# A linear-attention kernel with a gated output: a new order table, engine choices and PSUM banks for the same operations

## The chip, the cores and the metric

The kernel runs on one core of one Trainium2 chip. The metric is the device time of one execution in microseconds (us), lower is better. A core has five engines that each work through a queue of their own in order: TensorE (PE in the profile, with its weight loads as PEld), VectorE (DVE), ScalarE (ACT), GpSimd (POOL) and SyncE (SP), the last used here for issuing transfers. They meet only through semaphores. An instruction whose semaphore is not yet there holds up everything behind it in its queue.

## The reference

Eight batches of attention with a feature map, then a gated linear layer:

```
proj = x @ w_phi;  proj -= max|proj|;  phi(x) = [exp(proj), exp(-proj)]     # for q and k, 64 -> 128 features
kv  = phi(k)^T v;   z = sum phi(k)                                          # per batch and head
x   = phi(q) kv / (phi(q) z + 1e-6)                                         # (8, 576, 512)
gate = sigmoid(causal convolution of x, 5 taps);  out = ((x @ w_val) * gate) @ w_out
```

There are 8 batches, 8 heads, 576 rows, head width 64. Inputs and output are float32, the kernel computes in bfloat16 with float32 accumulation.

## The kernel before, in words

The kernel keeps everything of a batch on the chip. The rows of a batch are cut into 18 chunks of 128, and these into five units (four of 4 chunks, one of 2). A Python function `build` lists the work of all batches as tasks (1064 of them): each has a kind, a batch, the engine or engines that can do it, and the group of PSUM banks that it opens or uses. `build` itself fixes no order. Three tables do that:

- `ORDER` is the list of task numbers in the order in which they are written out. Each engine's queue is that list, cut down to the engine's own tasks.
- `FLEX` gives the engine (A, D or P for ACT, DVE, POOL) of each task that more than one engine can do, in order of task number.
- `BANKS` gives the PSUM banks, of 8, of each group. A group of two banks is read as one two-row block.

`WARM` adds idle matmuls (a 128x512 product of ones that nobody reads, L481) ahead of the places of `ORDER` that it names ("place:bank:count"), and before the change there are also 14 `warm` tasks of two such matmuls each. The durations in `build` (0.44, 2.22 and so on) are a planner's; nothing reads them when the kernel is built.

The stages of one batch, with the lines of the profile:

| stage | TensorE | who takes it on |
|---|---|---|
| k | `kp`: projection of kT (L555) | DVE maximum MK (L562), ACT two exps per unit into KTIL (L572), then `ek`: ACT exp of the maxima (L581) |
| v, kv | `st`: 36 matmuls per call, four calls (L598) | before it `vs`: v times EK into VT (L588, L589; 4 per batch, POOL or DVE); after it `kv`: copy of the sums (L606 DVE, L610 ACT) |
| q | `qm`: projection of qT (L555), `mqt`: transpose (L631), `qp`: projection again, minus the maximum (L642, L649) | DVE maximum MQP (L562), `mqr` (L634), ACT two exps per unit into QTIL or QTT (L657, L660) |
| x | `num`: five per batch (L670, L677), `xtp`: transposes (L699, L703) | DVE `nrm` (L688, L691), `xtc` copy into XT (L711, L716), POOL `halo` (L720) |
| gate, val | `gate` (L732, L739), `val` (L751) | ACT `tanh` (L743), DVE `gv` (L757), POOL `gvc` (L763) |
| out | `out` (L775) | `oev`: ACT (L612) or DVE (L608), store issued on SP (L797 and following) |

TensorE works with four shapes of its array here: 128x128 (`num`, `out`, transposes, idle matmuls), 64x128 (`kp`, `qm`, `qp`, `st`, `val`), 128x64 (first part of `gate`, the small fifth `num` and third `xtp`) and 64x64 (second part of `gate`).

Batches overlap: while batch b is in its gate and out stages, b+1 is in its x stage and b+2 in its k and q stages. The opening is different. k and q of batch 0 come as float32 in pieces through SP, and TensorE transposes them (`tp32`, L514). k and q of batch 1 are two transfers that POOL's queue issues (L528), q first, then k, then `w_val` (L445), then q of batch 2; they land in the tile QTIL as bfloat16, and TensorE transposes them too (`tp16`, L533). From batch 2 on the transposes are transfers (L543). In POOL's queue before the change stand, behind these loads: `c_eb` (L442), the first two `vs` of batch 0 with the load of k of batch 2 between them, the gate's weights `c_gt` (L472 to L477), the other two `vs` of batch 0, then batch 1.

In TensorE's queue before the change the transposes of k of batch 1 stand behind all five `qm` of batch 0, behind three of its `qp` and four `qm` of batch 1.

Of the kernel before, what the change touches and what calls it, by code (L numbers as in the profile page):

```python
# [25 lines left out]
PEB = 1  # L26
XB = (6, 7)
NO = 6
NW = 14
NJ = 2 * NC  # L30
XH = R // 2
HALO = 16
XW = HALO + XH
WARM = (
    "8:7:5 21:7:1 214:5:1 "
)
STD = 1.18
E1 = D + 1
QW = 2 * NR

ORDER = (
    "15 16 18 17 20 19 22 21 24 35 23 37 26 25 36 39 57 27 38 59 41 32 34 170 40 43 61 60 33 172 55 42 73 74 64 47 171 174 58 "
    "193 311 49 63 44 0 28 76 62 56 50 29 48 65 93 75 45 94 67 53 91 66 54 30 46 92 51 68 97 173 31 89 98 77 188 90 184 52 "
    "185 95 194 96 69 186 189 72 79 5 187 99 228 2 71 100 229 104 313 190 105 70 226 80 9 106 227 101 78 1 103 234 191 110 "
    "175 235 192 10 111 230 178 102 182 179 183 107 112 231 180 108 195 312 11 181 232 109 84 233 81 197 203 82 206 196 6 85 "
    "113 83 314 204 198 8 7 114 199 12 201 319 236 237 205 86 200 320 115 238 202 207 87 210 4 88 116 239 208 315 14 240 118 "
    "117 316 209 211 119 122 212 128 317 241 129 215 242 123 217 124 318 214 125 120 130 213 176 131 243 321 216 329 121 13 "
    "332 3 322 126 331 177 127 132 218 324 330 354 433 434 219 323 355 247 221 248 435 139 220 352 140 353 250 141 436 252 "
    "358 359 149 222 251 249 325 437 150 133 327 356 134 357 244 438 135 246 360 361 223 326 245 333 224 439 136 225 328 137 "
    "265 335 362 266 142 138 363 334 337 143 145 144 338 336 151 339 367 152 440 369 146 253 340 370 254 441 368 267 268 255 "  # L50
    "341 259 442 372 269 256 261 343 260 364 371 443 262 147 366 444 342 148 450 365 446 447 263 452 154 449 445 451 166 155 "
    "257 264 562 448 563 258 458 565 167 344 459 453 347 485 564 345 461 273 346 274 486 454 460 348 455 270 275 477 478 162 "
    "456 271 566 481 457 158 482 163 479 272 480 376 159 349 377 160 483 284 484 378 156 462 350 161 464 285 373 465 351 157 "
    "276 374 567 463 277 487 286 466 488 568 375 467 279 278 492 569 287 379 493 280 153 380 288 281 468 570 494 282 289 164 "
    "573 283 571 577 575 391 472 578 295 576 299 392 165 296 574 393 572 579 290 469 685 686 394 300 606 470 580 607 395 381 "
    "688 471 495 687 382 385 473 496 307 386 497 608 308 581 383 583 609 387 303 584 388 489 304 384 689 291 491 582 389 490 "
    "292 498 604 390 499 474 605 475 500 585 476 610 588 405 611 399 406 690 400 586 410 407 401 691 396 587 411 501 397 612 "
    "503 414 692 613 398 502 589 402 415 591 614 403 693 408 590 404 615 293 592 616 409 593 297 510 618 595 301 506 511 168 "
    "412 617 507 294 696 413 622 298 699 729 812 813 516 730 302 624 425 416 169 594 517 504 623 814 426 421 698 505 518 619 "
    "422 519 815 508 621 697 599 512 429 620 513 727 816 430 509 628 596 629 520 431 728 731 600 630 597 694 625 732 598 735 "  # L60
    "432 627 514 736 417 626 515 712 733 418 695 715 601 734 714 700 602 702 713 521 603 524 703 522 817 527 523 701 525 528 "
    "530 526 818 529 531 704 532 737 705 708 819 537 711 738 707 539 538 820 709 535 706 305 540 633 710 427 536 739 423 716 "
    "533 634 309 740 722 306 631 534 741 748 428 632 856 750 745 424 935 857 541 643 746 635 936 310 644 639 723 747 636 542 "
    "937 640 749 751 645 637 646 753 938 558 543 638 647 752 823 559 717 854 862 641 826 863 939 546 855 825 724 718 642 547 "
    "860 725 861 554 726 824 742 555 858 744 719 859 827 720 743 828 940 651 721 648 941 652 649 662 653 650 754 829 419 663 "
    "654 548 755 830 831 556 655 832 756 942 420 656 766 549 864 833 767 760 757 557 550 834 865 943 835 761 821 768 837 660 "
    "544 769 560 551 758 770 661 838 869 759 657 870 836 822 664 944 871 866 665 658 868 762 666 763 659 867 872 545 667 979 "
    "873 839 980 764 561 677 842 945 765 874 673 678 840 981 674 780 982 843 675 771 841 850 781 679 772 985 782 774 986 552 "
    "676 773 977 775 978 950 680 776 777 844 953 954 553 778 955 785 779 952 669 786 668 951 783 845 670 956 671 789 784 957 "
    "875 672 790 849 983 877 846 984 946 847 876 787 848 949 878 788 851 880 947 962 791 879 852 965 804 853 948 963 958 987 "  # L70
    "805 883 959 964 796 988 966 884 881 960 972 893 882 887 797 894 889 961 885 888 992 973 989 994 886 890 798 895 800 896 "
    "991 891 799 808 801 993 897 968 892 974 967 990 1001 975 1002 998 976 681 1003 809 999 969 682 810 995 1000 970 907 996 "
    "971 904 908 997 905 792 811 909 1004 906 1006 1005 793 1012 1007 1010 1016 1013 1008 916 1011 898 1009 1017 1014 901 917 "
    "1018 899 902 1019 910 1015 903 794 900 1020 806 914 683 911 795 912 802 807 1024 913 684 1021 915 803 1025 1027 1026 "
    "1030 1028 1031 1022 1029 923 1032 1037 924 1023 925 1033 1039 926 1034 1035 1040 1038 927 919 928 1036 931 929 920 1041 "
    "1054 932 918 921 930 1046 933 1055 922 1058 1056 1047 934 1042 1048 1059 1062 1057 1060 1050 1043 1049 1051 1044 1063 "
    "1052 1061 1045 1053 "
)
FLEX = (
    "ADAADAAAAAPPAPPDAAAADDAADAPPDPPDDAAADPPDPPDDADAPPAPPDAAAAAPPAPPDAADDPPAPPAAADADPPDPPDDADAPDDPPADDDDA"  # L80
)
BANKS = (
    "460006544445500124166757234523230145452301456767723672301674501445674652345230145234501276045505450101236723016701016767"
    "674230145670101011236736601674501014523236503323016723674501454567232370123456723450124567741230123236745236732374567452"
    "323450123452367010016767230167676452322367450167016767453636623674567452301452301454500101010101232320101732014501676767"
    "010122154523230145674545676767454450145674545450012303223672301010145236636423236745456701010145014524523670167452323457"
    "201230145450123457466234567014567230123674545701672301672345230177674501234545016744555"
)


# [66 lines left out]
def build(plan, em=None):  # L157

    def fn(name, *a):
        if em is None:  # L160
            return None
        f = getattr(em, name)
        return lambda t: f(t, *a)

    A = plan.add
# [5 lines left out]

    ceb = A("lv", 0, 0, "POOL", 2.6, fn("c_eb"), rank=-800)
    hold = None

    for i in range(NW):
        A("warm", 0, i, "PE", 0.44, fn("warm2"), [], plan.group("warm", 1), 0)

    for b in range(B):

# [122 lines left out]
        for c in range(5):  # L302
# [5 lines left out]
            if c in (1, 3, 4):  # L308
                i = c // 2
# [43 lines left out]
class Emit:  # L353
# [125 lines left out]

    def warm(self, bank):  # L480
        self.nc.tensor.matmul(self.PS[:, bank, :], self.ONES[:, 0:P], self.ONES[:, :], start=True, stop=True)  # L481

    def warm2(self, t):
        for _ in range(2):
            self.warm(t.grp.banks[0])

    def hold(self, t, u):
        self.nc.gpsimd.tensor_copy(self.HOLD[:, :], self.XN32["k"][:, u * 9 * D:u * 9 * D + 1])
# [317 lines left out]
@with_exitstack  # L806
def kernel(
    ctx: ExitStack,
    tc: tile.TileContext,
    q: bass.AP,  # L810
    k: bass.AP,
    v: bass.AP,
    w_phi: bass.AP,
    moe_w_val: bass.AP,
    moe_conv_w: bass.AP,
    moe_w_out: bass.AP,
    out: bass.AP,
):
    nc = tc.nc
    with tc.manual_schedule(engines=None):  # L820
        em = Emit(nc, tc, ctx, q, k, v, w_phi, moe_w_val, moe_conv_w, moe_w_out, out)
        plan = build(Plan(), em)
        warm = {}
        for x in WARM.split():
            i, bank, n = x.split(":")
            warm[int(i)] = (int(bank), int(n))
        for i, t in enumerate(plan.follow()):
            for _ in range(warm[i][1] if i in warm else 0):
                em.warm(warm[i][0])
            if t.fn is not None:  # L830
                t.fn(t)
# [30 lines left out]
```

## Time and profile before

| | |
|---|---|
| time, three runs | 229.36, 230.55 (median), 231.44 us |
| the profiled execution: its span, first to last instruction | 233.1 us |
| its own time | the page gives no other than the span |
| instructions | 9168 |
| busy: PE, DVE, ACT, POOL | 211.9 (91%), 176.4 (76%), 181.7 (78%), 103.0 us (44%) |
| mean granted TensorE clock | 0.990 |
| transfers | 39.87 MB, mean 171 GB/s |

Busy time is the union of an engine's instructions. For TensorE it counts the time from a matmul's start to its modelled end, and these overlap, so a busy TensorE need not be one at its peak; the time from one task's start to the next one's start says more. In timelines a row merges neighbours of one kind: start in us from the span's start, us taken, engine, line, operation, output<-inputs, how many, and in brackets the idle time just before with what ended it.

### The profile page before, as it was taken

The numbers are of one execution on the slowest core, as the hardware profiler recorded it, in microseconds if no ns is written. First come the engines' busy times: TensorE is split into PE (matmuls) and PEld (weight loads), VectorE is DVE, ScalarE is ACT, GpSimd is POOL, SyncE is SP. The second block draws the span as 40 slices with busy tenths as digits, with TensorE's granted clock in tenths as the row PEclk, the third lists the DMA queues.
The fourth block names the chain that finished last, engine by engine and source line by source line (L and its number), as shares of the span: only waits on it lengthen the run. The fifth ranks groups of instructions, "written<-read, shape, count | busy, mean of one in ns | idle before, by whom it ended". The sixth has DMA issues, their size and how long they took to land.

```text
span 233.1 us, 9168 instructions
## 1 busy us (share of the span) xinstructions
PE 211.9 (91%) x4027; PEld 145.5 (62%) x4027; DVE 176.4 (76%) x264; ACT 181.7 (78%) x267; POOL 103.0 (44%) x158
## 2 busy tenths in 40 slices
PE   7888997699998999999998599999999999999990
PEld 3566555567676576666766367676665867676640
DVE  2569776998789877998899549796888899583361
ACT  2878999799899987998898479978998999913320
POOL 2715992694059329800495006940009739100020
PEclk9999999999999999999999979999999999999999
DMA  6999935999699779968999981969984106156156
GB/s 199 338 257 272 208 55 160 209 181 174 116 207 242 127 160 178 302 114 114 229 167 296 167 232 30 148 126 229 263 277 143 52 3 139 37 83 204 45 177 184
DMA packets 49426, 39.87 MB, mean 171 GB/s; under 512 B 33706, under 2 KB 38826, under 8 KB 49322
## 3 DMA queue, kind: packets, MB, share of 16 engines
q1 hardware_dynamic: 43136, 29.63, 52.4%
q0 software_dynamic: 5760, 9.31, 23.8%
q8 instruction: 31, 0.51, 0.8%
q10 hardware_dynamic: 490, 0.35, 0.5%
q14 instruction: 9, 0.07, 0.1%
HBM read 30.49 MB, written 9.44 MB: 171 GB/s over the span
## 4 chain that ended last, share of the span: by engine, by line
PE 59%; DVE 16%; DMA 6%; POOL 5%; issue 5%; ACT 4%; ACTq 1%; SPq 1%; DVEq 0%
PE PS L751 12%; PE PS L775 10%; PE PS L732 7%; PE PS L555 7%; PE PS L598 6%; DVE MK L562 4%; DMA kT<-KQN 4%; DVE XN L691 4%; PE PS L670 3%; DVE MQP L562 3%; PE PS L739 3%; POOL VT L588 3%; PE PS L642 3%; DMA KTIL<-in_k_dram 2%; DVE GV L757 2%
## 5 line engine op out<-in xcount | busy, mean ns | idle before, releaser
L588 POOL TENSOR_TENSOR VT<-VN,EK 128x1152 bf16<-128x1152 f32 x31 | 65.9, 2125 | 66.5 <-ACT EK L581 55.5
L572 ACT ACTIVATE KTIL<-PS 128x1024 bf16<-128x1024 f32 (+1 forms) x80 | 72.4, 946 | 6.5 <-PE PS L555 4.3
L657 ACT ACTIVATE QTIL<-PS 128x1024 bf16<-128x1024 f32 x64 | 62.5, 1035 | 3.7 <-PE PS L649 3.3
L562 DVE TENSOR_REDUCE MQP<-PS 128x8 f32<-128x1024 f32 (+1 forms) x40 | 44.2, 1113 | 6.6 <-PE PS L555 5.5
L562 DVE TENSOR_REDUCE MK<-PS 128x8 f32<-128x1024 f32 (+1 forms) x40 | 43.9, 1111 | 4.4 <-PE PS L555 4.0
L751 PE MATMUL PS<-XT,WV 64*128 64x288 bf16 x512 | 35.5, 283 | 0.4 <-DVE XN L691 0.2
L757 DVE SCALAR_TENSOR_TENSOR GV<-TH,PS 128x576 bf16<-128x576 bf16 x32 | 23.7, 752 | 15.4 <-PE PS L751 10.5
L743 ACT ACTIVATE TH<-PS 128x576 bf16<-128x576 f32 x32 | 20.2, 654 | 16.6 <-PE PS L739 16.4
L775 PE MATMUL PS<-WOUT,GV 128*128 128x512 bf16 x128 | 31.7, 380 | 0.0
L751 PEld LDWEIGHTS <-WV 64*128 64x128 bf16 x512 | 24.8, 94 | 8.0 <-issue 2.4
L598 PE MATMUL PS<-VT,KTIL 64*128 64x65 bf16 x1152 | 24.5, 191 | 5.1 <-issue 3.5
L598 PEld LDWEIGHTS <-KTIL 64*128 64x128 bf16 x1152 | 21.4, 95 | 8.0 <-issue 5.2
L691 DVE TENSOR_TENSOR XN<-PS,RCP 128x512 bf16<-128x512 f32 x32 | 22.1, 692 | 1.1
L732 PE MATMUL PS<-XT,GF 128*64 128x288 bf16 x256 | 21.5, 301 | 0.3 <-DVE MQP L562 0.2
L670 PE MATMUL PS<-KV,QTIL 128*128 128x65 bf16 x512 | 20.1, 193 | 1.5 <-DVE GV L757 0.5
L670 PEld LDWEIGHTS <-QTIL 128*128 128x128 bf16 x512 | 18.2, 97 | 5.0 <-issue 2.7
L612 ACT ACTIVATE OUTS<-PS 128x512 f32<-128x512 f32 x22 | 13.3, 605 | 9.6 <-PE PS L775 9.1
L775 PEld LDWEIGHTS <-GV 128*128 128x128 bf16 x128 | 11.0, 97 | 11.6 <-issue 1.1
L720 POOL COPY XT<-XT 128x224 bf16<-128x224 bf16 x8 | 3.0, 375 | 34.2 <-DVE XT L716 22.3
L555 PE MATMUL PS<-W,kT 64*128 64x128 bf16 x288 | 15.4, 225 | 2.8 <-ACT kT L522 1.0
L732 PEld LDWEIGHTS <-GF 128*64 128x64 bf16 x256 | 13.2, 112 | 4.5 <-issue 2.0
L555 PE MATMUL PS<-W,qT 64*128 64x128 bf16 x288 | 15.1, 222 | 0.8 <-ACT TH L743 0.6
(76 smaller groups left out, 265.6 us busy)
## 6 DMA issues: line engine op xcount, KB each, us to landing
VN<-in_v_dram SPq DMA_DIRECT2D x8, 1152.0 KB, 6.9
out_dram<-OUTS SPq DMA_DIRECT2D x31, 256.0 KB, 3.2
KQN<-in_q_dram POOLq DMA_DIRECT2D x6, 576.0 KB, 6.8
KQN<-in_k_dram POOLq DMA_DIRECT2D x6, 576.0 KB, 8.0
KTIL<-in_k_dram SPq DMA_DIRECT2D x4, 288.0 KB, 4.1
KTIL<-in_q_dram SPq DMA_DIRECT2D x4, 256.0 KB, 4.2
out_dram<-OUTS SPq DMA_DIRECT2D x14, 64.0 KB, 2.8
QTIL<-in_q_dram POOLq DMA_DIRECT2D x1, 576.0 KB, 9.4
```

Source lines behind the costliest of these rows:

```text
L555: nc.tensor.matmul(self.PS[:, t.grp.banks[par], i * P:(i + 1) * P], X[rows, (c0 + i) * P:(c0 + i + 1) * P], self.W2[rows, :], start=True, ...
L562: self.nc.vector.tensor_reduce(o, self.two(t.grp, n * P).rearrange("p a (c f) -> p a c f", f=F), AX.X, ALU.max, apply_absolute_value=True)
L572: self.nc.scalar.activation(self.KTIL[b % 2][:, s, c0:c0 + n, :, :].rearrange("p c a f -> p a c f"), self.two(t.grp, n * P).rearrange("p a ...
L588: eng.tensor_tensor(self.VT[g][:, s, :, 0:D], self.VN[b % 2][:, NC * g:NC * g + NC, :], e.to_broadcast([P, NC, D]), ALU.mult)
L598: nc.tensor.matmul(self.PS[:, t.grp.banks[ab], (s * 2 + x) * E1:(s * 2 + x + 1) * E1], self.KTIL[b % 2][rows, s, J // 2, J % 2, :], self.V ...
L657: self.nc.scalar.activation(o, i, AF.Exp, scale=1.0 - 2.0 * s)
L670: nc.tensor.matmul(self.PS[:, t.grp.banks[h // 4], (h % 4) * E1:(h % 4 + 1) * E1], Q[:, s, c % 2, h, (c // 2) * P:(c // 2 + 1) * P], self. ...
L691: nc.vector.tensor_tensor(o.rearrange("p (g h) d -> p g h d", g=ng), n[:, :, :, 0:D], rc.unsqueeze(3).to_broadcast([P, ng, 4, D]), ALU.mult)
L732: self.nc.tensor.matmul(self.PS[h2 * D:(h2 + 1) * D, t.grp.banks[par], 0:R], self.GF[:, h, i, :], X[:, h, :, HALO - 8 * s:HALO - 8 * s + X ...
L751: nc.tensor.matmul(self.PS[:, t.grp.banks[par], 0:R], self.WV2[rows, h, j * P:(j + 1) * P], X[rows, h, :, HALO:XW], start=(h == 0), stop=( ...
L757: nc.vector.scalar_tensor_tensor(out=self.GV[b % 3][:, j, :, :], in0=self.TH[j][:, :, :], scalar=1.0, in1=self.two(t.grp, R), op0=ALU.add, ...
L775: nc.tensor.matmul(self.PS[:, t.grp.banks[0], :], lhsT, self.WOUT[:, j, :], start=(j == 0), stop=(j == 3))
```

## The change

The operations stay the same, and so do the functions that write them out. New are:

- `ORDER`, for the same tasks without the 14 `warm` tasks (1050 tasks; their numbers shift by 14).
- `FLEX`: the copies of transposed k and q of batch 0 and 1 go 10 to DVE and 6 to ACT (before 5 and 11), all 32 `vs` to POOL (before 31, one to DVE), `kv` 9 to DVE and 7 to ACT (before 10 and 6), `oev` 13 to DVE and 23 to ACT (before 14 and 22; one of DVE's is shared between both).
- `BANKS`: a group of two is now any two banks (0 and 5, 1 and 6), before always neighbours (0 and 1, 2 and 3).
- `WARM`: 14 idle matmuls at five places, where there were 35 (7 in `WARM`, 28 in `warm` tasks).

In TensorE's queue the last transposes of k of batch 1 (units 16 to 18 and 8 to 16 of its chunks) now stand behind the `kp` and one `qm` of batch 0 and all its transposes but one, ahead of the other four `qm` of batch 0, of their transpose and of all `qp`. In POOL's queue the load of k of batch 2 moves ahead of `c_eb`, and the four `vs` of batch 0 stand together, ahead of `c_gt`. In SP's queue the two transposing transfers of batch 2 move ahead of the load of v of batch 2. At the end, the eviction of the last `out` goes to ACT, behind the other last evictions and the two stores that ACT issues.

```diff
-NW = 14
...
 WARM = (
-    "8:7:5 21:7:1 214:5:1 "
+    "3:0:6 107:5:3 125:0:2 136:6:2 159:5:1 "
 )
 ORDER = (
-    "15 16 18 17 20 19 22 21 24 35 23 37 26 25 36 39 57 27 38 59 41 32 34 170 40 43 61 60 33 172 55 42 73 74 64 47 171 174 58 "
...
+    "1 2 3 10 4 5 12 6 7 8 9 20 21 23 24 156 158 160 11 43 45 46 25 26 14 22 13 15 18 19 44 27 47 49 297 51 54 16 17 35 299 "
+    "52 59 60 50 48 36 29 30 41 31 28 39 32 179 61 33 34 53 55 58 40 57 79 80 159 168 169 0 166 167 62 37 38 56 64 83 84 197 "
...
 FLEX = (
-    "ADAADAAAAAPPAPPDAAAADDAADAPPDPPDDAAADPPDPPDDADAPPAPPDAAAAAPPAPPDAADDPPAPPAAADADPPDPPDDADAPDDPPADDDDA"
+    "ADDDDADAADPPDPPDADAADADDADPPDPPADADADPPAPPADAAAPPDPPAAADAAPPAPPDADADPPAPPDDADDDPPAPPDAAAAPPDPPDAADAA"
 )
 BANKS = (
-    "460006544445500124166757234523230145452301456767723672301674501445674652345230145234501276045505450101236723016701016767"
...
+    "014454450523670167232405350301141432534160513351722405662041627162704045740307540470671316275604352624253401035360517273"
...
-    for i in range(NW):
-        A("warm", 0, i, "PE", 0.44, fn("warm2"), [], plan.group("warm", 1), 0)
...
-    def warm2(self, t):
-        for _ in range(2):
-            self.warm(t.grp.banks[0])
```

## The prediction

> **What bounds the kernel now.** I read first the page's busy slices (each digit is the busy tenths of 5.8 us), then the shares of the chain that ended last.
>
> ```profile
> PE   7888997699998999999998599999999999999990
> ...
> DVE  2569776998789877998899549796888899583361
> ACT  2878999799899987998898479978998999913320
> ...
> PEclk9999999999999999999999979999999999999999
> ...
> PE 59%; DVE 16%; DMA 6%; POOL 5%; issue 5%; ACT 4%; ACTq 1%; SPq 1%; DVEq 0%
> ```
>
> TensorE is full from about 75 us on, DVE and ACT are nearly full up to slice 35, and the chain runs mostly over TensorE. Next, the timeline of TensorE, for what a task really takes from its start to the next one's start:
>
> ```profile
> 196.14 0.75 PE L598 MATMUL PS<-VT,KTIL 64*128 64x65 bf16 x36
> 196.73 0.27 PE L642 MATMUL PS<-qT,W 64*128 64x256 bf16 x2
> ...
> 200.33 0.75 PE L598 MATMUL PS<-VT,KTIL 64*128 64x65 bf16 x36
> 201.02 1.17 PE L732 MATMUL PS<-XT,GF 128*64 128x288 bf16 x16
> ```
>
> The same 36 matmuls take 0.59 us ahead of a task of the same array shape and 0.69 ahead of another shape. All kinds show this step: `out` 0.86 and 0.96, `kp` 0.22 and 0.33, `val` 0.98 and 1.09. So a change of shape costs 0.10 us. Counted in the order of the built program, TensorE changes shape 204 times before and 167 times after.
>
> With such start-to-start times, where nothing waits, I add up each queue: full `kp` and `qm` 0.22, `qp` 0.44, `st` 0.58, `num` 0.49, `val` 0.98, `out` 0.86, `gate` 0.51+0.15, big transposes 0.44, an idle matmul 0.215, each shape change 0.10; ACT's exps 0.90 (short ones about 0.5), DVE's maxima 1.13 and 0.60, `nrm` 0.84, `gv` 0.66. TensorE has 196.7 us of work before and 188.5 after, ACT 170.8 and 170.2, DVE 168.3 and 165.6. TensorE is the bound, with some 10% of room on ACT and DVE.
>
> I cut the run at the end of `num` of batch 1 (L670, 67.5 us). From there TensorE has 147.3 us of work and is done at 227.6: 160.1 us, 12.8 of them lost. The largest loss is one hole:
>
> ```profile
> 128.38 0.67 PE L598 MATMUL PS<-VT,KTIL 64*128 64x65 bf16 x31
> 131.92 0.25 PE L598 MATMUL PS<-VT,KTIL 64*128 64x65 bf16 x5 [2.87 <-issue]
> ```
>
> TensorE stops inside a task for 2.9 us with nothing to wait for that the profile shows, and then runs at half clock for 3.4 us (the 7 in PEclk): about 4.7 us. The rest, 8.1, is small waits. That hole may be this execution's own. Its span alone, 233.1 us, is above the runs' median of 230.55, and above the slowest run. I work out a difference against 233.1, take the hole as equal on both sides, and apply the difference to the median.
>
> **Part 1: the opening, +8.0 us.** The new order puts the transposes of k of batch 1 ahead of four `qm` and every `qp` of batch 0. When does that k land? From the page's issues and the timeline:
>
> ```profile
> QTIL<-in_q_dram POOLq DMA_DIRECT2D x1, 576.0 KB, 9.4
> QTIL<-in_k_dram POOLq DMA_DIRECT2D x1, 576.0 KB, 17.5
> WV<-in_moe_w_val_dram POOLq DMA_DIRECT2D x1, 512.0 KB, 18.7
> ...
> 8.41 0.75 POOL L528 DMA_DIRECT2D QTIL<-in_k_dram  x1
> ...
> 26.73 0.56 PEld L533 LDWEIGHTS <-QTIL 128*128 128x128 bf16 x10
> ```
>
> Issued at 8.41 it lands at 25.9; before, the transposes stood far enough back to run at 26.7 and did not wait. The change leaves every transfer ahead of it as it was (pieces of k and q, two loads of v, q), so I keep 25.9. In the new queue TensorE reaches these transposes at about 14 us: its work up to there is 8.0 us, plus the waits of the old opening. ACT and DVE have copies of those transposes early in their queues and block as well, by about 16 us. By 25.9 the old order has done all maxima of batch 0 and three of the exps of its q; the new one has one of the maxima of q and no exp of it.
>
> From 25.9 on, the new queues in order. ACT resumes at 27.1 with the copy. From it to the last exp of q of batch 0 stand 15.5 us (8.3 of them q exps of batch 0, 4.6 k exps of batch 1 that now stand ahead of them); about 1.2 us more go to waiting for the maximum of q, as DVE does its part only now. So these exps end at 43.8, before at 37.2. The `kp` that needs their banks stands in front of two `st`, so these end near 45.2, their copy on DVE at 46.5, and `num` of batch 0 begins near 47 (before 39.1). ACT's next 20.6 us, to the copy of batch 1's sums, end at 64.4; DVE then has 10.6 us up to the last `nrm` of batch 1. So `num` of batch 1 ends near 75.5 (67.5 before): +8.0. POOL doesn't decide: four `vs` from 29.1 at 2.2 us each, with 0.7 of waiting, end at 39.0.
>
> Bounds: k lands between its neighbours in POOL's queue, q at 17.1 and `w_val` at 27.8. That makes part 1 -0.8 to +9.9. I keep 25.9, its own row.
>
> **Part 2: TensorE's work behind that point, -5.1 us.** 147.3 becomes 142.2. Shape changes left fall from 139 to 112, 2.7 us. The other 2.4 us is work that the new order has done by then: a `val`, a `qp`, two and a half `kp`, a transpose.
>
> **Part 3: losses behind that point, +1.0 us.** Between the ends of `num` of batches 1 and 5 TensorE's queue held 91.4 us against ACT's 79.2 before; after it is 82.9 against 79.2. The cover for ACT's delays shrinks from 12.2 to 3.7. Bounds from the old run: 2.7 us lost in 140 to 220 us and 4.9 in 60 to 120 give 4.8 and 11.6 us over 142, against the 8.1 without the hole: -3.3 to +3.5. I take +1.0, as the margin is more like the second stage's.
>
> **Part 4: the end, +1.3 us.** Before, the last two evictions are on DVE and ACT with the stores spread:
>
> ```profile
> 226.59 1.49 ACTq L803 DMA_DIRECT2D out_dram<-OUTS  x2
> 228.18 0.38 ACT L782 ACTIVATE OUTS<-PS 128x256 f32<-128x256 f32 x1 [1.62 <-DVE OUTS L781]
> 228.59 0.57 ACTq L795 DMA_DIRECT2D out_dram<-OUTS  x1
> ```
>
> The last store is issued 3.2 us after the matmuls of the third last `out` end (225.9). After the change a whole eviction (0.60) and its store on SP (0.56) stand behind these three, all in one row: 0.6+1.5+0.4+0.6+0.6+0.6 and gaps make 4.5 us. Bounds 0 to +1.6.
>
> **Costed at nothing.** The 21 idle matmuls taken out (4.5 us of TensorE): nearly all stand in 1 to 47 us, where the next task waits for ACT, DVE or a transfer. All `vs` on POOL: batch 7's four take 8.8+0.3 us after `ek` where the old split took 8.6, and TensorE has 13 us of queued work over that stretch. Earlier transposing transfers of batch 2: they wait for k at 33.4 and end near 42, ahead of the delayed rest; without the delay they would gain up to 4 us. Copies moved between ACT and DVE: under 2 us on each, inside the delay.
>
> **Sum.** 8.0 - 5.1 + 1.0 + 1.3 = +5.2 us: a span of 238.3 instead of 233.1, a time of 235.8 instead of 230.55.
>
> **Rivals.** *The new order runs dense* (not slower). The place is ACT's and DVE's queues from 26 us on. My +8.0 holds some 4 us of waits that I put together by hand. DVE's queue alone, from 26.2 without a wait, reaches the last `nrm` of batch 1 after 45.1 us, at 71.3: +3.8. With losses behind at the best old rate (-3.3) the sum is 3.8-5.1-3.3+1.3 = -3.3: 227.3. It breaks even when these waits and losses together come out 5.2 us below mine. For it: the order is drawn from measured durations, and ACT's queue is short enough. Against it: the thin margin of part 3.
>
> *k comes earlier.* Below a landing at 20.7 us the wait no longer costs more than the rest gains; at q's 17.1 the sum is -3.6: 227.0. Nothing that shares the transfers moves, so this is unlikely.
>
> *Half clock stays.* The rows show TensorE slow at first whatever PEclk says: 8 matmuls of L555 took 0.61 us at 13.0 and 0.40 at 18.8. After the 10 us hole it starts slow again. If it stays so up to the first `num`, its 14.3 us of queued work there take 28.6, 7 more than the time there is: 242.8. For it: the idle matmuls that filled this stretch are mostly gone. Against it: in the row above 3.4 us at half clock was all that a hole cost. The Trainium skill (TensorE: Matmul & The Clock Gate, What's actually happening) says that an idle window of about 3.4 us halves the clock and that only a sustained busy one restores it. The hole above, 2.9 us and then half clock, agrees with the first half of it. By that rule the slow stretch could last as long as TensorE keeps waiting; one run of matmuls, as before, would end it.
>
> **How the numbers follow.** The sum above 0.57 (own range 232 to 241), dense order 0.25, earlier k 0.06, half clock 0.12. A measurement of this kernel tells about 1% (2.3 us) from no change. Dense order and earlier k give most of faster (0.21), their upper ends and the lower end of the sum give same (0.15), the rest is slower (0.64). The range reaches from the dense case to the half clock: 227 to 243.
>
> **What would show it.** Right: TensorE, ACT and DVE all idle from about 16 to 26 us and released by the transfer of k; q exps of batch 0 ending near 44; `num` of batch 1 ending near 75; TensorE needing 150 us from there. Wrong: no hole at 16 to 26, or `num` of batch 1 ending before 71, or fewer than 145 us behind it.

## The result, and the profile after

| | before | after |
|---|---|---|
| time, median of 4 runs each | 229.96 us (229.26 to 231.44) | 531.03 us (528.05 to 532.2) |
| profiled execution: span | 233.1 us | 530.4 us |
| busy PE, DVE, ACT | 211.9, 176.4, 181.7 us | 313.6, 180.6, 189.7 us |
| mean granted TensorE clock | 0.990 | 0.627 |

After against before is a ratio of 2.307 (95% interval 2.295 to 2.319). The forecast was 235.8 us, range 227 to 243. Direction right, size not at all. The ratios of experiments 1, 5 and 6 leave out executions more than 1.5% above the fastest of their kernel, so they can differ from the ratio of the medians. In the changed kernel's profile a line number is that of before less 9 (less 5 up to L476).

From the page of the changed kernel, the busy slices that answer to those shown of before (one digit is now 13.3 us):

```profile
PE   7136455544477666555575566765555656557784
...
DVE  5252232423334442332343323333333332223430
ACT  6142543432235432423244434143331341342223
...
PEclk9555555555557676556568655685576665557898
```

No engine is full anywhere, and that from the first slices to the last. DVE and ACT do the same work in about the same time (4 and 8 us more) and wait for the rest. TensorE is busy 102 us longer: its mean granted clock is 0.627, so each matmul takes longer (L742 `val` 381 ns on average, 283 before). It still stands idle for 217 of 530 us. The chain of waits is of no use here: it breaks off after 2% of the span.

The exps of k, from the page of before and then from that of the changed kernel, show the same busy time and the same mean, and the idle time ahead of them grown from 6.5 to 101.6 us:

```profile
L572 ACT ACTIVATE KTIL<-PS 128x1024 bf16<-128x1024 f32 (+1 forms) x80 | 72.4, 946 | 6.5 <-PE PS L555 4.3
L563 ACT ACTIVATE KTIL<-PS 128x1024 bf16<-128x1024 f32 (+1 forms) x80 | 72.4, 938 | 101.6 <-PE PS L546 33.0
```

The wait that the prediction was about is there, and it is small. The timeline just behind it shows what is not in the prediction:

```profile
25.08 1.25 PE L524 MATMUL PS<-ident,QTIL 128*128 128x128 bf16 x10 [10.65 <-DMA QTIL<-in_k_dram]
...
27.91 0.69 DVE L553 TENSOR_REDUCE MQP<-PS 128x4 f32<-128x512 f32 x1 [0.97 <-ACT KTIL L563]
...
28.65 0.61 PE L546 MATMUL PS<-W,kT 64*128 64x128 bf16 x8 [0.83 <-DVE MQP L553]
...
29.03 0.31 PE L546 MATMUL PS<-W,qT 64*128 64x128 bf16 x1
29.36 2.00 ACT L563 ACTIVATE KTIL<-PS 128x1024 bf16<-128x1024 f32 x3 [0.78 <-PE PS L546]
30.43 0.58 PE L546 MATMUL PS<-W,qT 64*128 64x128 bf16 x7 [1.09 <-ACT KTIL L563]
...
31.12 1.23 DVE L553 TENSOR_REDUCE MQP<-PS 128x8 f32<-128x1024 f32 x1 [1.92 <-PE PS L546]
...
32.39 0.61 PE L546 MATMUL PS<-W,qT 64*128 64x128 bf16 x8 [1.38 <-DVE MQP L553]
```

Read the three engines in turn. The `kp` of unit 3 of batch 1 (28.65) starts when DVE ends a maximum of q of batch 0 (27.91 + 0.69 = 28.60). The next `qm` does one matmul at 29.03 and its other seven at 30.43, behind an exp of k on ACT. The `qm` after it (32.39) starts when DVE ends the maximum before (31.12 + 1.23 = 32.35). None of these tasks needs the other's data, and none shares a bank with it: `kp` writes banks 2 and 7, the maximum read 1 and 4; the first `qm` writes 0 and 3, the exp read 2 and 7; the second `qm` writes 1 and 4, the maximum read 0 and 3. Each pair of banks lies across the other. The split `qm` shows the edge: its first matmul goes to bank 0, outside of 2 to 7, and runs; its second goes to bank 3, inside, and waits. The engines work one after another, in steps of about a microsecond, and the busy slices stay low to the end of the run.

Over the whole run the waits of TensorE add up from many short ones (us in total, times, longest):

```profile
PE PS L546 <- ACT KTIL L563: 11.7, 10, 2.0
PE PS L524 <- DMA QTIL<-in_k_dram: 10.7, 1, 10.7
PE PS L742 <- DVE MK L553: 10.6, 5, 3.9
```

`val` (L742) reads XT and WV and needs no maximum of k, yet waits 10.6 us for one. In one of the five cases (1.4 us) the maximum had read the very banks that `val` then writes. In the other four (9.3 us) they share no bank. The longest:

```profile
401.18 0.36 PE L742 MATMUL PS<-XT,WV 64*128 64x288 bf16 x1
...
404.19 1.23 DVE L553 TENSOR_REDUCE MK<-PS 128x8 f32<-128x1024 f32 x1 [2.00 <-ACT QTIL L648]
405.46 0.90 PE L742 MATMUL PS<-XT,WV 64*128 64x288 bf16 x6 [3.93 <-DVE MK L553]
```

This `val` writes banks 0 and 4, the maximum reads 2 and 5. Its first matmul goes to bank 0 and runs; its second goes to bank 4, between 2 and 5, and waits.

The semaphore waits in the built programs say the same. Before, of 849 waits of tasks with PSUM banks, 7 are for a task that neither gives them data nor shares a bank (false waits, from here on). After it is 379 of 813.

**Theory 1.** A group of two is read as one strided access, `PS[:, a:b+1:b-a]`. The software that places the semaphores takes it as an access to all banks from a to b. With neighbours that is exact. With banks 2 and 7 it is six banks, and a task waits for every user of 3 to 6 as well. **Theory 2:** the new order of the tasks starves the engines. **Theory 3:** with too few idle matmuls TensorE falls to half clock and stays there. **Theory 4:** banks far apart are slow for the chip itself.

### The profile page after: what moved, and what is told of

Read it like the earlier page. It is cut to its first block, busy times and chain, and to the rows that moved or that the text cites. A ratio compares the mean times of both kernels' runs of the same rounds, so it can differ in the third digit from the quotient of the medians.

```text
span 530.4 us, 9138 instructions
## 1 busy us (share of the span) xinstructions
PE 313.6 (59%) x4006; PEld 204.0 (38%) x4006; DVE 180.6 (34%) x265; ACT 189.7 (36%) x264; POOL 104.6 (20%) x160
## 5 line engine op out<-in xcount | busy, mean ns | idle before, releaser
L563 ACT ACTIVATE KTIL<-PS 128x1024 bf16<-128x1024 f32 (+1 forms) x80 | 72.4, 938 | 101.6 <-PE PS L546 33.0
L553 DVE TENSOR_REDUCE MQP<-PS 128x8 f32<-128x1024 f32 (+1 forms) x40 | 44.2, 1116 | 75.0 <-PE PS L546 37.3
L742 PE MATMUL PS<-XT,WV 64*128 64x288 bf16 x512 | 56.9, 381 | 21.3 <-DVE MK L553 10.6
L742 PEld LDWEIGHTS <-WV 64*128 64x128 bf16 x512 | 35.8, 123 | 36.5 <-issue 25.1
L766 PE MATMUL PS<-WOUT,GV 128*128 128x512 bf16 x128 | 45.8, 511 | 5.1 <-ACT KTIL L563 1.3
L589 PE MATMUL PS<-VT,KTIL 64*128 64x65 bf16 x1152 | 34.1, 230 | 24.5 <-ACT QTIL L648 7.2
L589 PEld LDWEIGHTS <-KTIL 64*128 64x128 bf16 x1152 | 31.5, 121 | 27.5 <-issue 14.6
L723 PE MATMUL PS<-XT,GF 128*64 128x288 bf16 x256 | 31.5, 390 | 16.9 <-DVE MQP L553 5.7
L661 PE MATMUL PS<-KV,QTIL 128*128 128x65 bf16 x512 | 28.9, 223 | 16.8 <-ACT QTIL L648 7.6
L633 PE MATMUL PS<-qT,W 64*128 64x512 bf16 (+1 forms) x80 | 24.0, 526 | 22.9 <-ACT QTIL L648 10.6
L546 PEld LDWEIGHTS <-qT 64*128 64x128 bf16 x288 | 14.4, 119 | 37.0 <-issue 36.7
L723 PEld LDWEIGHTS <-GF 128*64 128x64 bf16 x256 | 18.7, 141 | 24.5 <-issue 20.6
L679 DVE RECIPROCAL RCP<-PS 128x8 f32<-128x8 f32 (+1 forms) x40 | 8.0, 201 | 57.2 <-PE PS L661 30.8
```

Source lines behind the costliest of these rows:

```text
L546: nc.tensor.matmul(self.PS[:, t.grp.banks[par], i * P:(i + 1) * P], X[rows, (c0 + i) * P:(c0 + i + 1) * P], self.W2[rows, :], start=True, ...
L553: self.nc.vector.tensor_reduce(o, self.two(t.grp, n * P).rearrange("p a (c f) -> p a c f", f=F), AX.X, ALU.max, apply_absolute_value=True)
L563: self.nc.scalar.activation(self.KTIL[b % 2][:, s, c0:c0 + n, :, :].rearrange("p c a f -> p a c f"), self.two(t.grp, n * P).rearrange("p a ...
L589: nc.tensor.matmul(self.PS[:, t.grp.banks[ab], (s * 2 + x) * E1:(s * 2 + x + 1) * E1], self.KTIL[b % 2][rows, s, J // 2, J % 2, :], self.V ...
L633: nc.tensor.matmul(self.PS[:, t.grp.banks[par], 0:n * P], self.W2[rows, :], X[rows, c0 * P:(c0 + n) * P].rearrange("p (y h x) -> p h y x", ...
L661: nc.tensor.matmul(self.PS[:, t.grp.banks[h // 4], (h % 4) * E1:(h % 4 + 1) * E1], Q[:, s, c % 2, h, (c // 2) * P:(c // 2 + 1) * P], self. ...
```

## The experiments

**1. Only the banks redrawn (e1_pairs).** ORDER and FLEX as changed; every group of two gets neighbours again, chosen along ORDER so that no live group shares a bank. The idle matmuls go to banks free at their places.

```diff
 BANKS = (
-    "014454450523670167232405350301141432534160513351722405662041627162704045740307540470671316275604352624253401035360517273"
+    "760010017145236723454501456767010152323010123232354523465670101012..."
```

> The new ORDER and FLEX kept, only BANKS drawn anew so that every two-bank group has neighbouring banks (0 1, 2 3, 4 5, 6 7) again. Theory 1 (a strided two-bank access over banks that are not neighbours is taken by the layer that sets the semaphores as an access to all banks between them, so that tasks on interleaved pairs wait for each other): the false waits are gone (8 of 875 waits of tasks with PSUM banks in the built program, against 379 of 813), so 220 to 245 us, mean clock above 0.95. Theory 2 (the new order of the tasks is what starves the engines): stays near 530 us. Theory 3 (too few idle matmuls, TensorE falls to half clock and stays there): stays above 400 us with a clock near 0.6.

Measured 245.1 us (241.8 to 248.4), 1.053 times before (1.045 to 1.060), clock 0.938. From its page:

```profile
PE   7721887988999988997999899979929999999990
...
PEclk9985579999999999997999999999977999999997
```

286 of the 301 us are gone with the bank numbers alone. The time lies at the upper edge of theory 1's 220 to 245, the clock a little below its 0.95. The order stays, so theory 2 falls; the 14 idle matmuls stay, so theory 3 falls as the cause: the half clock followed from the waits. It is also the kernel that the prediction had in mind, and its terms can be read there (below).

**2. Only the banks spoiled, in the kernel before (e2_far, e3_half).** All pairs four apart, then only half of them and two apart:

```diff
-    0 1   2 3   4 5   6 7      # the pairs of before
+    0 4   1 5   2 6   3 7      # e2_far
+    0 2   1 3   4 5   6 7      # e3_half
```

> The kernel before with its bank numbers relabelled and nothing else: the four pairs 0 1, 2 3, 4 5, 6 7 become 0 4, 1 5, 2 6, 3 7. Order, engines, idle matmuls and every true conflict of banks stay. In the built program 774 of 967 waits of tasks with PSUM banks are then on a task that shares no bank with them (before 7 of 849). Theory 1: 400 to 560 us, engines idle everywhere, clock well below 0.9. Theories 2 and 3 (order, idle matmuls): 230 us, as both are those of before.

> The kernel before with half of the relabelling: the pairs 0 1 and 2 3 become 0 2 and 1 3, the pairs 4 5 and 6 7 stay. 220 of 869 waits of tasks with PSUM banks are then on a task that shares no bank with them (7 of 849 before, 774 of 967 when all pairs are interleaved four apart, which took 635 us). Theory 1: a time between, 260 to 380 us. A theory in which only pairs in different halves of the banks cost something (that chip feature would spare 0 2 and 1 3): 230 us.

Measured 635.0 us (clock 0.577) and 311.0 us (0.926), one run each. TensorE's busy slices of e2_far look like those of the changed kernel:

```profile
PE   5555445555545655564666555555565664566665
```

A relabelling that leaves every real conflict as it was makes the old kernel 2.75 times as long, with none of the new order in it. The time grows with the false waits: 7, 220, 774 of them make 230, 311, 635 us. e2_far is above its expectation of 400 to 560; TensorE is busy 361.6 us there against 211.9, at its low clock. In e3_half the interleaved pairs are only two apart, so "far apart" isn't the condition: lying across each other is.

**3. The same banks, read one at a time (e4_split).** ORDER, FLEX, BANKS and WARM of the changed kernel.

```diff
-        self.nc.scalar.activation(KTIL[:, s, c0:c0+n, :, :]..., self.two(t.grp, n * P)..., AF.Exp, ...)
+        for a in range(2):
+            self.nc.scalar.activation(KTIL[:, s, c0:c0+n, a, :], self.PS[:, t.grp.banks[a], 0:n * P]..., AF.Exp, ...)
     # and so for the maxima, qexp, tanh, nrm, gv, kv
```

> The changed kernel with its ORDER, FLEX, BANKS and WARM as they are, but every read of a two-bank group written as two instructions of one bank each (exps, maxima, tanh, nrm, gv, kv). No access spans a bank that it does not touch. That adds some 230 instructions to ACT and 250 to DVE, each about 0.1 us by the difference of the short and the long exps and maxima, so 20 to 25 us of work on either engine, of which part is hidden. Theory 1: 235 to 270 us. Theory 2 (order) and theory 3 (clock): still about 530 us. A fourth theory, that banks far apart are themselves slow to read or write on the chip, would also leave it near 530, and its single instructions would be longer for the same elements.

Measured 244.0 us (one run), clock 0.951. Bank numbers and queues are those of the 531 us kernel; only the form of the reads differs. So it isn't the banks, and not their distance, but the one access across them. Nor is that access slow on the chip itself (theory 4): in the changed kernel the two-bank exps of k take 938 ns on average, before 946, and the maxima 1116 and 1113. And the waits stand in the built program (379 of 813 false ones), so the chip doesn't make them. ACT has 447 instructions instead of 264 and DVE 450 instead of 265, for 189.7 and 185.8 us of busy time.

**4. The kernel before without its 35 idle matmuls (e5_noidle).**

> The kernel before without its 35 idle matmuls, order, engines and banks kept. Theory 1 and the prediction (they lie beside waits and cost or bring nothing much): 228 to 234 us. Theory 3 (the idle matmuls are what holds the clock): the clock stays at half over the opening and beyond, 240 us or more.

Measured 233.1 us, 1.010 times before (1.007 to 1.014), clock 0.975. What theory 3 is worth here is 2.3 us: `num` of batch 1 ends at 69.2 instead of 67.5.

**5. What is left of the loss (e6_swap, e7_xpose, e8_all).** All start from e1_pairs. Its timeline has two large holes of TensorE:

```profile
23.59 1.25 PE L524 MATMUL PS<-ident,QTIL 128*128 128x128 bf16 x10 [9.38 <-DMA QTIL<-in_k_dram]
...
181.61 0.82 PE L546 MATMUL PS<-W,qT 64*128 64x128 bf16 x12 [4.42 <-DMA qT<-KQN]
```

The second is a transposing transfer that came late. SP's timeline shows why:

```profile
166.20 1.42 SPq L500 DMA_DIRECT2D VN<-in_v_dram  x2
167.74 9.09 SPq L534 DMA_TRANSPOSE kT<-KQN  x1
176.94 2.75 SPq L534 DMA_TRANSPOSE qT<-KQN  x1
```

SP's queue stood until 166.1 us at a store whose eviction was late; two loads of v followed, and beside them the issue of the transposing transfer of k took 9.1 us, where such a row takes 2.7 to 6.1 at other places.

```diff
 # e6_swap: POOL's queue           # e7_xpose: SP's queue
-load q1, load k1                  -store (3, 2), load v6, load v7, transpose k7, transpose q7
+load k1, load q1                  +transpose k7, transpose q7, store (3, 2), load v6, load v7
 # e8_all: both, and the eviction of the last out in FLEX: A -> D
```

> The changed kernel with neighbouring banks (245.1 us, TensorE idle 9.4 us for k of batch 1 at 23.6), and two entries of ORDER swapped: POOL issues the load of k of batch 1 ahead of that of q. k should then land near 17 and q near 24 to 26. If the opening loss is the wait for the second of the two transfers, as the prediction has it: the 9.4 us hole is gone, a smaller wait for q of 1 to 4 us stands later, num of batch 1 ends at 69 to 72 instead of 75.2, and the time falls by 4 to 7 us, to 238 to 241. If the opening is limited by ACT's and DVE's work instead, num of batch 1 stays at 74 to 76 and the time within 2 us.

> The changed kernel with neighbouring banks, and in SP's queue the two transposing transfers of k and q of batch 7 moved ahead of one store (that of chunk 2 of batch 3's out) and two loads of v that stood before them. If TensorE's 4.4 us wait at 177.2 and the half clock after it (the two slices at 7) come from that place in SP's queue: both gone, num of batch 6 ends at 200 to 203 instead of 208.4, time 238 to 242. If something else sets that stretch (ACT or DVE): 243 to 247.

> The changed kernel with neighbouring banks, the swap of the two loads, the moved transposing transfers, and the last eviction on DVE instead of ACT. If the three losses are separate: 245 less 5, less 5, less 1, so 232 to 236. If they hide each other, 237 to 242.

Measured 242.6 (ratio 1.047, 1.039 to 1.055), 237.5 (1.028, 1.022 to 1.034) and 234.4 us (1.013, 1.006 to 1.019).

e6_swap brought less than expected. Issued first, k doesn't land near 17 us but at 21.2; the hole shrinks only to 7.0 us and `num` of batch 1 ends at 73.7:

```profile
21.19 1.25 PE L524 MATMUL PS<-ident,QTIL 128*128 128x128 bf16 x10 [6.99 <-DMA QTIL<-in_k_dram]
```

e7_xpose did what its first theory said: the 4.4 us hole and the half clock behind it are gone, `num` of batch 6 ends at 199.4 instead of 208.4, a little more than expected. e8_all fits separate losses; its middle, 234.4, is still above before.

**6. The opening undone (e9_open, e10_late).** The first 400, or 680, entries of ORDER with their engines, banks and idle matmuls from before, the rest in the new order, neighbouring banks throughout.

> The opening undone: the first 400 entries of ORDER with their engines, banks and idle matmuls are those of the kernel before (past num of batch 1), the rest follows in the changed kernel's order with its engines, with the moved transposing transfers and the last eviction on DVE, and neighbouring banks. If the prediction's opening term is right and separable (k of batch 1 costs some 8 us, the rest gains): no hole near 15 to 25 us, num of batch 1 ends at 67 to 69, and with the 160 us that the version with moved transfers took from there to its end, a span of 227 to 230 and a time of 228 to 232. If the new order behind it only gains because the delayed opening let other engines get ahead (that is, the delay is given back later): 233 to 238.

> The same with the cut at entry 680 (after num of batch 3): so only the last batches are in the changed kernel's order, again with neighbouring banks. From the end of num of batch 3 the kernel before took 111.7 us to the end of its span, with one hole of 2.9 us and the half clock behind it; the version with moved transfers took 116.1 from there. If the gain of the new order lies in the middle batches: no gain is left, 230 to 236. If it lies in the last ones: 226 to 229.

Measured 236.4 (1.024, 1.018 to 1.030) and 231.9 us (1.0035, 1.0003 to 1.0067). In e9_open the hole is gone and `num` of batch 1 ends at 69.9, 5.6 us ahead of e7_xpose; at the end of `num` of batch 2 only 0.9 of that is left (95.8 against 96.7). The time is 1.1 us below that of e7_xpose, about what the last eviction on DVE alone brings (1.2 us less behind the last matmul). So the second expectation holds, 233 to 238. Mine of 228 to 232 took over the 160 us that e7_xpose needs from `num` of batch 1 on, but e7_xpose has done more work by then: TensorE has 145.3 us left in e9_open against 141.5. In the profiled execution of e9_open it also loses 17.1 on the way against 11.6, but that execution took 239.5 us, 3.1 above its median, and 4.3 of the 5.5 us are holes with the mark "issue" (6.7 in three holes against 2.4 in one), of the kind told of in the last section. In e10_late no gain is left, its first expectation.

**7. Idle matmuls into the hole (e11_busy).** From e8_all:

```diff
-    "3:0:6 107:4:3 125:6:2 136:6:2 159:0:1 "
+    "3:0:6 66:0:28 107:4:3 125:6:2 136:6:2 159:0:1 "
```

> The version with neighbouring banks, swapped loads, moved transposing transfers and the last eviction on DVE (234.4 us), plus 28 idle matmuls (28 x 0.215 = 6.0 us at full clock) in TensorE's queue just ahead of the transposes of k of batch 1, where it stands idle for 6.0 us. If the half clock behind that hole (matmuls of 8 at 0.61 to 0.68 instead of 0.40 up to about 31 us) costs time: the granted clock stays at full from 14 us, num of batch 1 ends 1 to 3 us earlier than 72.25, time 231 to 233.5. If ACT and DVE set the opening (they hold the work behind the hole): num of batch 1 ends within 0.5 us of 72.25 and the time within 1 us of 234.4.

The clock is held behind the hole (the ten transposes of L524 there take 0.72 us at 21.1, in e8_all 1.25 at 20.6), and `num` of batch 1 ends at 72.1 instead of 72.25: on that point the second expectation, ACT and DVE set the opening. But the time isn't within 1 us: of six runs two took 236.1 and 236.7 us, four 240.2 to 242.0 (median 240.4). The profiled one, the shortest, has the same span as that of e8_all, 234.3. What makes the others longer stays open.

## Why the prediction was wrong, by its own steps

**The step that failed: BANKS has no term.** The prediction counts queues, shape changes, landings and cover; the new banks are neither in a part nor under "costed at nothing". Its start-to-start model lets a task wait for its data and for the users of its own banks, which holds before (7 false waits) and not after (379). What it left out is worth 286 us: 531.0 against 245.1 in e1_pairs. It could have been read without the chip: I counted shape changes in the built program and didn't ask whom its waits wait for.

**"Half clock stays" as a rival** had the right sign and the wrong root: one hole in the opening, 242.8 us. In e1_pairs, where that hole stands alone, matmuls are slow up to about 33 us and no longer. In the changed kernel the mean clock is between 0.58 and 0.62 in each stretch of 100 us up to 500 us. The Trainium skill (TensorE: Matmul & The Clock Gate, What's actually happening) has it that only a sustained busy window of some 3.4 us brings the full clock back. The trace goes with that in the main: of the changed kernel's 145 stretches without a pause of over 0.25 us only 25 are longer than 3.4 us. The idle window of about 3.4 us that the prediction names was not needed: its hole was 2.9 us long, and e2_far, whose longest pause is 3.0 us, has a mean clock of 0.577. Over the runs the clock falls with TensorE's busy share: 91% and 0.990 (before), 84% and 0.938 (e1_pairs), 76% and 0.926 (e3_half), 59% and 0.627 (changed), 57% and 0.577 (e2_far). Where between 76 and 59% it gives way, and by what rule, no run shows. The clock isn't a cause of its own, as it came back with the banks. It is a part of the price: TensorE's busy time is 109 us longer than in e1_pairs (313.6 against 204.4), its idle time 177.

**The four terms**, read in e1_pairs, which has the new order without the false waits (its profiled execution, span 244.5, is 11.4 us above before's 233.1; the spans of its four runs are 240.0 to 246.6, so the third row may hold some us that are this execution's own):

| term | forecast | measured |
|---|---|---|
| 1: `num` of batch 1 ends | 75.5 (+8.0) | 75.2 (+7.7) |
| 2: TensorE's work behind it | 142.2 (-5.1) | 141.2 (-6.1) |
| 3: losses behind it, with holes | 13.8 (+1.0) | 20.8 (+8.0) |
| 4: last matmul to end of span | +1.3 | 6.6 for 5.4 (+1.2) |

Term 1 came as worked out, with its path: the exps of q of batch 0 end at 43.1 (forecast 43.8), `num` of batch 0 begins at 46.2 (near 47). That it fits to 0.3 us is in part luck: k landed at 23.6 instead of 25.9, and the path behind it took 2 us longer than forecast. Terms 2 and 4 are right within 1 us (the four leave 0.6, the gap at the cut). The sign "TensorE needing 150 us from there" doesn't follow from the prediction's own terms, which give 156.0 (142.2 and 13.8); it took 162.7. The end runs in one row, as forecast; the changed kernel, behind its last matmuls at 523.8:

```profile
524.41 0.39 ACT L773 ACTIVATE OUTS<-PS 128x256 f32<-128x256 f32 x1 [1.62 <-DVE OUTS L772]
524.82 0.57 ACTq L786 DMA_DIRECT2D out_dram<-OUTS  x1
525.49 0.60 ACT L603 ACTIVATE OUTS<-PS 128x512 f32<-128x512 f32 x1 [0.70 <-DMA out_dram<-OUTS]
526.12 0.56 SPq L788 DMA_DIRECT2D out_dram<-OUTS  x1
```

Shape changes cost what the prediction read; the same 36 matmuls of `st` in e1_pairs, first ahead of their own shape (0.58 to the next start), then ahead of another (0.67):

```profile
107.42 0.74 PE L589 MATMUL PS<-VT,KTIL 64*128 64x65 bf16 x36
108.00 0.39 PE L546 MATMUL PS<-W,qT 64*128 64x128 bf16 x8
108.22 0.74 PE L589 MATMUL PS<-VT,KTIL 64*128 64x65 bf16 x36
108.89 0.68 PE L723 MATMUL PS<-XT,GF 128*64 128x288 bf16 x7
```

Term 3 is mis-sized by 7 us in that execution. I priced the thinner cover of ACT's delays, and left out SP's queue, which the change also reorders for batch 7: before, both transposing transfers of batch 7 stand ahead of the loads of v of batches 6 and 7, after they stand behind both. e7_xpose moves those two transfers: the losses come to 11.6, below before's 12.8, and the span to 235.8 where the sum said 238.3.

**What the sum got wrong in kind:** it gives back too little of the +8.0. e9_open takes 5.6 us of it away and gains nothing, since the delayed opening leaves 3.8 us less work behind; that the losses behind it are smaller as well isn't shown, as most of that difference is holes of one execution. Part 2 credits 2.4 us of such work. A term read at a cut is a price only with the work on its far side.

**Costed at nothing:** the idle matmuls; in the kernel before their removal costs 2.3 us (e5_noidle), which removes all 35 of them, so the cover that the prediction named was not whole.

**Rivals.** "The new order runs dense" (227.3) wasn't reached even with neighbouring banks: e7_xpose comes near its losses (11.6 against 9.5) but not near its opening. "k comes earlier" isn't what happened: k landed at about 25.1 in the changed kernel and 23.6 in e1_pairs, earlier than 25.9 but well behind that rival's 20.7; and its bound, q's 17.1, was no bound, as e6_swap shows k at 21.2 when issued in q's place. No version tried beats the kernel before.

## What to carry to other kernels

When a change renames buffers or banks, list whom each wait of the built program is for and whether the two share anything real; counts of instructions and waits don't show it (there were fewer waits after). Keep what one strided access spans next to each other, or split the access: with the extra instructions of e4_split the kernel took 244.0 us, with neighbouring banks 245.1, with the false waits 531.0. When all engines are half idle in every slice, look for pairs of tasks on different engines that start at each other's end without common data, before looking at order or clock.

## What the runs showed of the hardware that was not expected

**Holes marked "issue" begin with a 16 KB packet of an instruction queue (q8).** The hole of 2.9 us in the kernel before has cousins in nearly every run, at other places each time. In e7_xpose, the timeline and then the queues in 158.5 to 159 us:

```profile
161.16 0.45 PE L661 MATMUL PS<-KV,QTIL 128*128 128x65 bf16 x9 [2.42 <-issue]
```

```profile
q8 instruction: 1, 0.02, 12.2%
```

The hole is 158.75 to 161.16; a 16 KB packet of the instruction queue starts at 158.73. In the profiles of before, e1_pairs and e4_split to e11_busy, each of the 17 holes over 1.2 us behind 40 us that no data wait explains begins between 0.5 us before and 1.2 us after the start of such a packet. There are 31 such packets in a run, and none to four have such a hole. By chance a hole would fall that near to a packet about one time in four (31 times 1.7 us of some 230). The Trainium skill (Runtime: NRT & Kernel Launch, Instruction fetch mechanics) says that the engines fetch instructions in 16 KiB blocks by a transfer queue of their own, and that the cost is mostly hidden. The size agrees, and "mostly" leaves out holes of 1.3 to 2.9 us and, behind the longest, 3.4 us of half clock. That the fetch causes the hole is argued from this coincidence; no run took it away.

**Being issued first gains k little.** k of batch 1 lands 14.3 to 17.5 us after its issue in the ten profiles where it is issued behind q (the row of before, which the prediction took, is the longest), and still 13.0 to 13.8 us after it in the three where it is issued ahead of q. q issued first takes 9.0 to 11.3. In e6_swap the transfer engines are busy for eight tenths and more of every slice from 5 to 30 us; that this is why k gains so little isn't shown.
